# The last six token chunks of a sorted-attention and expert kernel, taken in pairs of 512 tokens

## The chip, the cores and the metric

The kernel runs on one core of a Trainium2 chip. Times are device microseconds of one execution. The profile is one further execution, recorded by the hardware profiler; its span runs from the first to the last instruction. In the texts PE is the matrix engine (TensorE), PEld its weight loads, DVE the vector engine, ACT the scalar engine, POOL GpSimd, and SP the engine whose queue issues most DMAs.

## The reference

Attention with sorted blocks comes first. Its result is the input of a layer of four experts, all of which see all tokens:

```python
# attention: q, k, v are (4, 8, 768, 64); P is an 8 x 8 Sinkhorn matrix per head
k_sorted = einsum('bhij,bhjcd->bhicd', P, k_blocks)      # v likewise
attn = softmax(scale * q_block @ k_sorted_block.T)       # within each block of 96
x = (attn @ v_sorted_block) as (3072 tokens, 512)

# experts: w1 is (4, 512, 1024), w2 is (4, 1024, 512)
p = domain_probs / (domain_probs.sum(-1, keepdims=True) + 1e-09)
for e in range(4):
    h = np.maximum(x @ w1[e], 0.0)
    out += p[:, e:e + 1] * (h @ w2[e])
```

## The kernel before

The 3072 tokens are taken in twelve chunks of 256, three for each of the four batches. A chunk goes through a first layer (x times w1, then Relu and the token's weight p, which gives the hidden values H in the buffer Hb) and a second layer (H times w2, summed over the four experts). The attention of batches 1 to 3 is woven into the chunks of the batch before. From chunk 6 on (G0 is 5, GN is 12) no attention is left, and all twelve matrices of input sums have been made, so TensorE has nothing but the two layers to do.

Both layers of these last chunks use Strassen's scheme in Winograd's form: a product of 2 x 2 blocks in seven block products in place of eight. In the second layer the two token blocks are the 128-token halves of a chunk, and the hidden values and the outputs are halved too. Sums of H blocks are made by the vector engine (h_sums, L747 to L753; into Sb, or in place over a block that is used up). In the first layer the blocks are two halves of 128 tokens, two halves of the 512 inputs and two halves of the 1024 hidden values. The sums on the weight side (s1, s3, n2, s4) were made earlier, in arena, in parts of Sb and over blocks of w1. Those on the token side (t1, n2, t3, t4) are four vector operations for each chunk, in token_sums (L1000), into the dead buffers kT and ET of the attention.

The function seven(g, e) returns the seven products of one expert as steps that are called by number. Each product has 4 blocks of 128 hidden values times 2 halves of the input, that is 8 matmuls of 128 columns, and fills one PSUM bank of 128 x 512 numbers. The product's line is L1047:

```python
dst[:, ds(f * P, P)], a[lhs][:, k, ds(f * P, P)], t[rhs][:, k, :],
```

Products are gathered in banks X, Z and Q. Product 1 goes to Z and is copied to X by ACT (L1067), since two sums start from it. Products 6 and 7 are added in X and copied out by ACT to u2 (L1074) and u3 (L1082). Product 2 completes Z and product 4 completes X, which the vector engine finishes with Relu and weight in one operation each (finish, L1053): these are the hidden values of the first token half. Product 3 and product 5 are in Q, to which the vector engine adds u3 (L1083) and u2 (L1091). ACT then takes the Relu (L1059) and GpSimd multiplies by the weight (finish2, L1060): these are the hidden values of the second token half.

The order on all engines is the order of the program (a manual schedule), written out in last_chunk (L1103 to L1217). An expert's step calls product 1 and 5 of its own, 2 and 6, with 7, 4 and 3 of the expert before among them. The second layer follows at L1161, and its products are the matmuls of L1150. The last steps of the first layer are called between its first products, and before its last product ends the next chunk has begun: token_sums(g + 1) at L1198 and last_begin(g + 1), with products 1 and 5 of the first expert, at L1203.

The weights p of a chunk are broadcast over the partitions by one DMA of 512 KB (load_p, L213) from SP's queue, issued at L1167, after the first product of the second layer. The tile pb has one buffer. Two output tiles, oa and ob, are taken for each chunk from a pool of two buffers (L1155). The first one to be written is oa, by the add at L1171. Stores are issued at L1206 (ob) and L1217 (oa), and for the last chunk also at L1173 and L1215.

last_tmp (L1015) lays the temporaries u2, u3, t22 and t12 into dead tiles: two buffers each for chunks 6 to 11. The transposed queries of the attention are in a pool tile qT with three buffers (L380).

Of the kernel before, what the change touches and what calls it, by code (L numbers as in the profile page):

```python
# [17 lines left out]
def kernel(  # L18
# [45 lines left out]

    state = {"n": 0}

# [181 lines left out]

    qTs = {}

    def warm(n):
# [127 lines left out]
    def st_q(b, pr):  # L379
        qT = att.tile([P, R, P], F16, name=f"qT_{b}_{pr}", tag="qT", bufs=3)  # L380
        nc.sync.dma_start_transpose(
            qT[:], natural[(b, "q")][:, pr].rearrange("p t h d -> p (t h d)")
        )
        qTs[(b, pr)] = qT.rearrange("p t x -> p (t x)").rearrange("p (i x) -> p i x", i=NB)
# [356 lines left out]

    def h_sums(e, which, own=False):
        blk = lambda kh, tok: Hb[:, homes.get(e, e), ds(kh * KH, KH), ds(tok * P, P)]
        sm = [Sb[:, n, e].rearrange("p (f x) -> p f x", f=KH) for n in range(4)]
        tt = nc.vector.tensor_tensor
        if which == 1:
            tt(sm[0], blk(0, 1), blk(1, 1), ALU.add)  # L747
        elif which == 2:
            tt(sm[1], sm[0], blk(0, 0), ALU.subtract)
        elif which == 3:  # L750
            tt(blk(0, 1) if own else sm[2], blk(0, 0), blk(0, 1), ALU.subtract)
        else:
            tt(blk(1, 0) if own else sm[3], blk(1, 0), sm[1], ALU.subtract)  # L753
# [231 lines left out]
    def token_sums(g, part=slice(0, 4)):  # L985
# [10 lines left out]
        for dst, x, y, op in (  # L996
# [3 lines left out]
            nc.vector.tensor_tensor(t[dst], t[x], t[y], op)  # L1000

    last = {}

    def last_banks(n):
# [10 lines left out]
    def last_tmp(g):  # L1015

        room = []
        if g > G0:
            t = moe.tile([P, NKC, NB, BLK], F16, name="tmp7", tag="xT").rearrange("p k i x -> p (k i x)").bitcast(F32)
            room += [t[:, ds(n * 512, 512)] for n in range(3)]  # L1020
        for m in range(2):
            t = att.tile([P, NB, 4, VW], F16, name=f"tmp7_{g}_{m}", tag="vs").rearrange("p i h w -> p (i h w)")
            t = t[:, 0:2048].bitcast(F32)
            room += [t[:, 0:512], t[:, 512:1024]]
        for m in range(1 if g > G0 else 2):
            t = att.tile([P, NB, 2, D], F16, name=f"tmp7x_{g}_{m}", tag="xsl").rearrange("p i h d -> p (i h d)")
            room.append(t.bitcast(F32))
        if g > G0:
            for n, nm in enumerate(("u2", "u3", "t22", "t12")):
                last[nm] = room[2 * n:2 * n + 2]  # L1030
        else:
            last["u2"] = last["t12"] = room[0::2]
            last["u3"] = last["t22"] = room[1::2]

    def seven(g, e):

        a, t, pb = As[e], Bs[g], pbs[divmod(g, R // 2)]
        n = e - (g == G0)
        X, Z = [last[nm][n % len(last[nm])][:] for nm in ("X", "Z")]
        u2, u3, t22, t12 = [last[nm][n % len(last[nm])] for nm in ("u2", "u3", "t22", "t12")]  # L1040
        Q = last["Q"][e if n == e else (0, 0, 1, 3)[e]][:]
        tt = nc.vector.tensor_tensor

        def product(dst, lhs, rhs, first=False):
            for f in range(KH):
                for k in range(2):
                    nc.tensor.matmul(  # L1047
                        dst[:, ds(f * P, P)], a[lhs][:, k, ds(f * P, P)], t[rhs][:, k, :],
                        start=(first and f == 0 and k == 0), stop=(f == KH - 1 and k == 1), skip_group_check=True,
                    )  # L1050

        def finish(i, j, src):
            nc.vector.scalar_tensor_tensor(  # L1053
                out=Hb[:, e, ds(i * KH, KH), ds(j * P, P)], in0=src.rearrange("p (f x) -> p f x", f=KH), scalar=0.0,
                op0=ALU.max, in1=pb[:, ds(e, 1), ds(j * P, P)].broadcast_to([P, KH, P]), op1=ALU.mult,
            )

        def finish2(i, j, src):
            nc.scalar.activation(src, src, AF.Relu, bias=0.0, scale=1.0)  # L1059
            nc.gpsimd.tensor_tensor(  # L1060
                Hb[:, e, ds(i * KH, KH), ds(j * P, P)], src.rearrange("p (f x) -> p f x", f=KH),
                pb[:, ds(e, 1), ds(j * P, P)].broadcast_to([P, KH, P]), ALU.mult,
            )
# [38 lines left out]

    def last_chunk(g, slot=None):  # L1103
        b, c = divmod(g, R // 2)
        final = g == GN - 1
        lead = int(g == G0)
# [13 lines left out]
        else:  # L1120
            last["e0"][2]()
            prs = {0: last["e0"]}
        for e in range(1 + lead, E):
            prs[e] = seven(g, e)
        for e in range(1 + lead, E):
            now, prev = prs[e], prs[e - 1]
# [11 lines left out]
        now[7]()  # L1138
        prev[12]()

        blk = lambda kh, tok: (lambda e, f: Hb[:, e, kh * KH + f, ds(tok * P, P)])
        sm = lambda n: (lambda e, f: Sb[:, n, e, ds(f * P, P)])
        bankB, bankA, bankC, bankQ = [last["Q"][n][:, 0:DH] for n in ((0, 2, 1, 3) if lead else range(4))]

        def product(ps, lhs, rhs, first=True, es=range(E), between=None, at=E - 1, part=ds(0, DH)):
            for e in es:
                if e == at and between:
                    between()
                for f in range(KH):
# [3 lines left out]
                    )  # L1153

        oa, ob = [moeo.tile([P, Dm], F32, name=f"{n}_{b}_{c}", tag="oacc") for n in ("oa", "ob")]  # L1155
        p1, p5, u2 = [moe.tile([P, DH], F32, name=f"{n}_{b}_{c}", tag=n, bufs=1) for n in ("p1", "p5", "u2")]
# [3 lines left out]

        product(bankA, blk(0, 0), "b11", between=now[4])  # L1161
        now[22]()
        nc.scalar.copy(p1[:], bankA)
        now[3]()
        now[12]()
        if not final:
            pbs[divmod(g + 1, R // 2)] = load_p(*divmod(g + 1, R // 2))  # L1167
        for e in range(E - 1):
            h_sums(e, 1)
        product(bankB, blk(1, 0), "b21")  # L1170
        tt(oa1, bankB, p1[:], ALU.add)  # L1171
        if final:
            nc.sync.dma_start(o[:, 2 * c, 0:DH], oa1)  # L1173
        h_sums(E - 1, 1)
        for e in range(E):
            h_sums(e, 2)
        product(bankC, blk(1, 1), "n4")
        nc.scalar.copy(ob1, bankC)
        for e in range(E):
            h_sums(e, 4, True)  # L1180
        if lead:
            for e in range(E):
                h_sums(e, 3, True)
            input_sums(0, 2, True)
# [6 lines left out]
        if not lead:  # L1191
            for e in range(E):
                h_sums(e, 3, True)
        early = 1 if final else 2
        for bank, part, _ in ends:
            product(bank[:, part], blk(1, 0), "b22", False, range(early), part=part)
        if not final:
            token_sums(g + 1)  # L1198
        product(bankA, blk(0, 1), "t3", False)
        if not final:  # L1200
            if lead:
# [7 lines left out]
        for bank, part, queue in ends:  # L1209
            product(  # L1210
                bank[:, part], blk(1, 0), "b22", False, range(early, E), None if final else last["e0"][6], 3, part
            )
# [127 lines left out]
    for g in range(G0 + 1):  # L1340
# [24 lines left out]
        else:  # L1365
            last_chunk(g, slot)
    for g in range(G0 + 1, GN):
        last_chunk(g)
# [28 lines left out]
```

## Time and profile before

| What | us |
|---|---|
| runs of the kernel | 363.46, 363.92, 370.13 (median 363.92) |
| the profiled execution | 362.61 |
| its span | 360.8 |
| PE busy | 353.0 |
| DVE busy | 277.3 |
| ACT busy | 173.6 |
| POOL busy | 133.9 |
| one chunk of the last six, in the trace | 24.70 |
| median time from issue to landing: weights p, stores of ob, stores of oa | 6.0, 2.0, 2.2 |

The page gives for every engine its busy time, and under it the share of each of 40 slices in tenths (9 is 90% or more); the PEclk row is TensorE's granted clock in tenths of full speed. The chain of work that ended last is followed back from the last instruction, at each step to what released it. A line of the timeline gives the start, the time until the last of the merged instructions ended, the engine, the line of the source, the operation, what it writes and reads, the count, and in brackets the idle time before and what ended it. Matmuls are pipelined, so their durations overlap, and the time of one is read from the distance of starts. A line of a stretch gives the stretch, its length, the busy time of PE, PEld, DVE, ACT and POOL with counts, the clock, the DMA share and the GB/s. Some matmul records can be missing from a trace.

### The profile page before, as it was taken

The numbers are of one execution on the slowest core, as the hardware profiler recorded it, in microseconds if no ns is written. First come the engines' busy times: TensorE is split into PE (matmuls) and PEld (weight loads), VectorE is DVE, ScalarE is ACT, GpSimd is POOL, SyncE is SP. The second block draws the span as 40 slices with busy tenths as digits, with TensorE's granted clock in tenths as the row PEclk, the third lists the DMA queues.
The fourth block names the chain that finished last, engine by engine and source line by source line (L and its number), as shares of the span: only waits on it lengthen the run. The fifth ranks groups of instructions, "written<-read, shape, count | busy, mean of one in ns | idle before, by whom it ended". The sixth has DMA issues, their size and how long they took to land.

```text
span 360.8 us, 10849 instructions
## 1 busy us (share of the span) xinstructions
PE 353.0 (98%) x4621; PEld 314.9 (87%) x4621; DVE 277.3 (77%) x561; ACT 173.6 (48%) x306; POOL 133.9 (37%) x148
## 2 busy tenths in 40 slices
PE   8799999999999999999999999999999999999996
PEld 8686857888888888988889899999999998999995
DVE  5653897779788777768878978869779679588695
ACT  2664430452324255368937257175283481571750
POOL 8872010466012330000626318147065082180470
PEclk9999999999999999999999999999999999999999
DMA  7999999999998999935995210210202203103101
GB/s 101 206 207 231 215 209 198 202 189 205 209 142 140 192 129 165 172 83 69 172 205 71 60 60 2 60 60 8 91 25 48 72 3 58 63 2 60 60 9 52
DMA packets 71964, 40.60 MB, mean 113 GB/s; under 512 B 40550, under 2 KB 66668, under 8 KB 71916
## 3 DMA queue, kind: packets, MB, share of 16 engines
q0 software_dynamic: 36560, 19.93, 41.0%
q1 hardware_dynamic: 35212, 19.92, 28.2%
q8 instruction: 36, 0.59, 0.7%
q14 instruction: 12, 0.10, 0.1%
q10 hardware_dynamic: 144, 0.07, 0.1%
HBM read 42.13 MB, written 6.34 MB: 134 GB/s over the span
## 4 chain that ended last, share of the span: by engine, by line
PE 91%; DVE 5%; ACT 1%; POOL 1%; issue 1%; DMA 0%; DVEq 0%; ACTq 0%; POOLq 0%
PE ps_Q L1150 24%; PE ps_h L777 18%; PE ps_X L1047 10%; PE ps_p L761 10%; PE ps_Z L1047 7%; PE ps_Q L1047 7%; PE ps_h L667 3%; PE ps_o L702 3%; PE ps_p L812 3%; PE ps_s L412 1%; PE ps_a L447 1%; PE ps_v L360 1%; PE ps_k L393 1%; PE ps_s L544 0%; DMA sn<-in_sort_net_dram 0%
## 5 line engine op out<-in xcount | busy, mean ns | idle before, releaser
L1060 POOL TENSOR_TENSOR Hb<-tmp,pb 128x512 f16<-128x512 f32 x40 | 50.7, 1275 | 84.7 <-ACT tmp L1059 83.3
L777 PE MATMUL ps_h<-xT,w 128*128 128x256 f16 x576 | 67.7, 273 | 0.0
L777 PEld LDWEIGHTS <-w 128*128 128x128 f16 x576 | 55.2, 98 | 7.3
L1150 PEld LDWEIGHTS <-Hb 128*128 128x128 f16 x576 | 53.8, 98 | 5.6
L783 DVE SCALAR_TENSOR_TENSOR Hb<-ps_h,pb 128x1024 f16<-128x1024 f32 x34 | 41.5, 1223 | 17.1 <-PE ps_h L777 16.8
L1047 PEld LDWEIGHTS <-w 128*128 128x128 f16 x864 | 52.4, 98 | 1.2 <-issue 0.3
L1150 PE MATMUL ps_Q<-w,Hb 128*128 128x256 f16 (+1 forms) x352 | 43.4, 268 | 0.0
L1047 PEld LDWEIGHTS <-arena 128*128 128x128 f16 x552 | 33.4, 98 | 0.1
L419 ACT ACTIVATE ET<-ps_s 96x768 f16<-96x768 f32 x24 | 18.0, 802 | 25.4 <-PE ps_s L412 25.1
L402 ACT CAST kT<-ps_k 64x384 f16<-64x384 f32 x48 | 22.7, 473 | 14.1 <-PE ps_k L393 13.1
L1047 PE MATMUL ps_X<-kT,arena 128*128 128x128 f16 x384 | 29.3, 219 | 0.0
L1067 ACT COPY ps_X<-ps_Z 128x512 f32<-128x512 f32 x27 | 15.4, 570 | 28.7 <-PE ps_Z L1047 28.3
L1083 DVE TENSOR_TENSOR tmp<-ps_Q,tmp 128x512 f32<-128x512 f32 x26 | 18.0, 691 | 14.2 <-ACT tmp L1082 10.0
L747 DVE TENSOR_TENSOR Sb<-Hb 128x512 f16<-128x512 f16 x45 | 27.7, 639 | 0.0
L1150 PE MATMUL ps_Q<-T,Hb 128*128 128x256 f16 x224 | 26.7, 273 | 0.0
L121 POOL DMA_DIRECT2D arena<-in_q_dram x24 | 19.9, 844 | 17.2 <-DMA qT<-arena 17.0
L1059 ACT ACTIVATE tmp<-tmp 128x512 f32<-128x512 f32 x40 | 25.4, 634 | 1.2 <-DVE tmp L1083 1.0
L761 PEld LDWEIGHTS <-Hb 128*128 128x128 f16 x232 | 21.9, 98 | 3.0
L1150 PEld LDWEIGHTS <-Sb 128*128 128x128 f16 x240 | 22.1, 98 | 2.4
L1074 ACT COPY tmp<-ps_X 128x512 f32<-128x512 f32 x26 | 15.2, 586 | 13.0 <-PE ps_X L1047 13.0
L1060 POOL TENSOR_TENSOR Hb<-tmp7x,pb 128x512 f16<-128x512 f32 x14 | 19.0, 1358 | 5.4 <-ACT tmp7x L1059 5.4
L1053 DVE SCALAR_TENSOR_TENSOR Hb<-ps_X,pb 128x512 f16<-128x512 f32 x27 | 18.4, 683 | 2.7 <-PE ps_X L1047 2.7
(206 smaller groups left out, 652.6 us busy)
## 6 DMA issues: line engine op xcount, KB each, us to landing
w<-in_moe_w_dram POOLq DMA_DIRECT2D x7, 1024.0 KB, 28.1
pb<-p_dram SPq DMA_DIRECT2D x12, 512.0 KB, 6.0
arena<-in_k_dram POOLq DMA_DIRECT2D x8, 384.0 KB, 9.4
arena<-in_v_dram POOLq DMA_DIRECT2D x8, 384.0 KB, 7.8
vs<-arena SPq DMA_DIRECT2D x36, 66.0 KB, 5.7
arena<-in_q_dram POOLq DMA_DIRECT2D x24, 96.0 KB, 8.4
out_dram<-ob SPq DMA_DIRECT2D x9, 256.0 KB, 2.0
out_dram<-oa SPq DMA_DIRECT2D x8, 256.0 KB, 2.2
```

Source lines behind the costliest of these rows:

```text
L121: nc.gpsimd.dma_start(t[:, h // 2, :, h % 2, :], q[b, h].rearrange("(t p) d -> p t d", p=P))
L402: nc.scalar.copy(kT[ds(D * hh, D), r], pk[ds(D * r, D), hh].rearrange("p a (i c) -> p a i c", c=CP),)
L419: nc.scalar.activation(ETs[2 * (pr % 2) + hh][:, 0:S].rearrange("c (a x) -> c a x", a=2), pss[hh][0:BLK, :, 0:HS], AF.Exp, bias=0.0, scale ...
L747: tt(sm[0], blk(0, 1), blk(1, 1), ALU.add)
L761: nc.tensor.matmul(ps, lhs(e, f), Ts[e][rhs][:, f, :], start=(first and e == es[0] and f == 0), stop=(done and e == es[-1] and f == KH - 1 ...
L777: nc.tensor.matmul(ps[:, f, :], w1sb[e][:, kc, ds((4 * g + f) * P, P)], xT[:, kc, ds(2 * c * P, 2 * P)], start=(kc == 0), stop=(kc == NKC ...
L783: nc.vector.scalar_tensor_tensor(out=Hb[:, homes.get(e, e), ds(4 * g, 4), :], in0=ps[:], scalar=0.0, op0=ALU.max, in1=weights(e).broadcast ...
L1047: nc.tensor.matmul(dst[:, ds(f * P, P)], a[lhs][:, k, ds(f * P, P)], t[rhs][:, k, :], start=(first and f == 0 and k == 0), stop=(f == KH - ...
L1053: nc.vector.scalar_tensor_tensor(out=Hb[:, e, ds(i * KH, KH), ds(j * P, P)], in0=src.rearrange("p (f x) -> p f x", f=KH), scalar=0.0, op0= ...
L1059: nc.scalar.activation(src, src, AF.Relu, bias=0.0, scale=1.0)
L1060: nc.gpsimd.tensor_tensor(Hb[:, e, ds(i * KH, KH), ds(j * P, P)], src.rearrange("p (f x) -> p f x", f=KH), pb[:, ds(e, 1), ds(j * P, P)].b ...
L1150: nc.tensor.matmul(ps, lhs(e, f), Ts[e][rhs][:, f, part], start=(first and e == 0 and f == 0), stop=(e == E - 1 and f == KH - 1), skip_gro ...
```

## The change

Chunks 6 to 11 are taken in pairs: (6, 7), (8, 9), (10, 11). In the first layer a pair is one block of 512 tokens, and its two token blocks are the two chunks. last_chunk is split into last_first (the first layer) and last_second (the second layer); a pair runs one last_first and then two last_seconds.

- seven(g, n) now stands for half an expert: expert n // 2 and two of the four blocks of hidden values. A product has 2 blocks times 2 input halves, 4 matmuls of 256 columns, and fills a bank of 512 as before. A pair has eight such steps. Chunk 5 (G0) keeps the 128-column form.
- The hidden values of the first chunk all come from the vector engine's finish and lie in Hb. Those of the second all come from ACT and GpSimd and lie in dead buffers: 2048 columns each of arena, of Sb's fourth part, of the query ring, and of an xT tile.
- pair_sums makes the four token sums once for each pair, with 512 elements in place of 256, at the place of token_sums in the second chunk's second layer.
- load_pair loads the weights of the first chunk with load_p and those of the second with two DMAs of 256 KB into xsl tiles. The extra DMAs are on SP's queue.
- last_tmp gives u2 with t12, and u3 with t22, three buffers each.
- The transposed queries go to a constant tile q_ring with three parts in place of the pool tile.
- The second last_second (upper) reads its blocks from the dead buffers, uses banks Z for two of its products, and has no steps of the first layer woven into its beginning.

The core of the diff:

```diff
 def st_q(b, pr):
-        qT = att.tile([P, R, P], F16, name=f"qT_{b}_{pr}", tag="qT", bufs=3)
+        qT = q_ring[:, state["q"] % 3]
+        state["q"] += 1
...
+    def pair_sums(g):
+        (x00, x10), (x01, x11) = halves(g)
+        own = lambda t: t[:, 0:4 * P].rearrange("p (k x) -> p k x", k=2)
+        t = Bs[g] = {
+            "b11": x00, "b12": x01, "b21": x10, "b22": x11,
+            "t1": own(kTs[0]), "n2": own(wide[0]), "t3": own(wide[2]), "t4": own(wide[3]),
+        }
...
+    def load_pair(g):
+        first, second = load_p(*divmod(g, R // 2)), []
+        b, c = divmod(g + 1, R // 2)
+        for n in range(2):
+            t = att.tile([P, NB, 2, D], F16, name=f"pb7_{g}_{n}", tag="xsl").rearrange("p i h d -> p (i h d)")
+            t = t.bitcast(F32).rearrange("p (e x) -> p e x", e=2)
+            nc.sync.dma_start(
+                t,
+                p_dram[ds(2 * n, 2), ds(b * S + 2 * c * P, 2 * P)].rearrange("(o e) x -> o e x", o=1).broadcast_to(
+                    [P, 2, 2 * P]
+                ),
+            )
+            second.append(t)
+        pbs[g] = lambda j, e: first[:, ds(e, 1), :] if j == 0 else second[e // 2][:, ds(e % 2, 1), :]
...
+            parts = (
+                arena[:, 4096:6144], Sflat[:, 6144:8192],
+                q_ring.rearrange("p n r x -> p (n r x)")[:, 0:2048], t[:, 0:2048],
+            )
+            last["H"] = [h.rearrange("p (f x) -> p f x", f=NFC) for h in parts]
...
+        last["u2"] = last["t12"] = room7[0::2]
+        last["u3"] = last["t22"] = room7[1::2]
...
+        else:
+            e, f0, cols = n // 2, n % 2 * 2, 2 * P
+            home = lambda i, j: (last["H"][e] if j else Hb[:, e])[:, ds(i * KH + f0, 2), :]
+            weight = lambda j: pbs[g](j, e)
+            Q = last["Q"][n % 4][:]
+        m = 512 // cols
...
-            for f in range(KH):
+            for f in range(m):
                 for k in range(2):
                     nc.tensor.matmul(
-                        dst[:, ds(f * P, P)], a[lhs][:, k, ds(f * P, P)], t[rhs][:, k, :],
+                        dst[:, ds(f * cols, cols)], a[lhs][:, k, ds((f0 + f) * P, P)], t[rhs][:, k, :],
...
+        N7 = E if lead else 2 * E
-        for e in range(1 + lead, E):
+        for e in range(1 + lead, N7):
             prs[e] = seven(g, e)
...
+    def last_second(g, now=None, upper=False):
+        closing = lead or upper
+        hb = (lambda e: last["H"][e]) if upper else (lambda e: Hb[:, e])
...
+        if upper:
+            bankA, bankB = last["Z"][1][:, 0:DH], last["Z"][0][:, 0:DH]
...
-        if not final:
-            token_sums(g + 1)
+        if closing and not final:
+            pair_sums(g + 1)
...
-    for g in range(G0 + 1, GN):
-        last_chunk(g)
+    for g in range(G0 + 1, GN, 2):
+        last_second(g, last_first(g))
+        last_second(g + 1, upper=True)
```

## The prediction

> **What bounds the kernel now.** I read the page first, for the engine that is never idle; then the chain that ended last; then busy times of the last chunks, for what one costs; then the timeline of one chunk, for the time per matmul and the slack of the engines behind TensorE.
>
> ```profile
> span 360.8 us, 10849 instructions
> PE 353.0 (98%) x4621; PEld 314.9 (87%) x4621; DVE 277.3 (77%) x561; ACT 173.6 (48%) x306; POOL 133.9 (37%) x148
> PE   8799999999999999999999999999999999999996
> PEclk9999999999999999999999999999999999999999
> PE 91%; DVE 5%; ACT 1%; POOL 1%; issue 1%; DMA 0%; DVEq 0%; ACTq 0%; POOLq 0%
> ```
>
> TensorE is busy from start to end at the full clock, and 91% of the chain is its matmuls. The stretches below are one chunk each (busy time by engine; x counts recorded instructions).
>
> ```profile
> 232.90:257.60 24.70, 24.70 (x338) 23.42 (x337) 19.43 (x40) 12.74 (x24) 10.32 (x8) 1.00 0.14 44
> 257.60:282.30 24.70, 24.70 (x338) 23.43 (x337) 19.43 (x40) 12.74 (x24) 10.32 (x8) 1.00 0.18 45
> ```
>
> TensorE has no gap in them. A change here gains only by fewer or cheaper matmuls, and loses what it makes TensorE wait. The time per matmul comes from TensorE's timeline, from starts far apart:
>
> ```profile
> 236.02 0.61 PE L1047 MATMUL ps_X<-kT,Sb 128*128 128x128 f16 x8
> ...
> 245.40 1.47 PE L1150 MATMUL ps_Q<-w,Hb 128*128 128x256 f16 x12
> ...
> 248.04 1.91 PE L1150 MATMUL ps_Q<-w,Hb 128*128 128x256 f16 x16
> ...
> 255.03 1.04 PE L1150 MATMUL ps_Q<-w,Hb 128*128 128x256 f16 x8
> ```
>
> From 236.02 to 245.40 lie 21 products of 8 first-layer matmuls: 9.38 / 168 = 55.8 ns each, 128 columns. From 248.04 to 255.03 lie 64 second-layer ones: 6.99 / 64 = 109.2 ns, 256 columns. So one of 256 is 2.4 ns cheaper than two of 128. The 219 and 273 ns of the groups are latencies of overlapped matmuls and are not used for the sum.
>
> One step of the first layer (about 3.13 us, one expert), all engines; the step begins at 238.70 with product 1 and the next at 241.83:
>
> ```profile
> 239.87 0.59 ACT L1082 COPY tmp<-ps_X 128x512 f32<-128x512 f32 x1
> 240.04 0.61 PE L1047 MATMUL ps_Z<-xT,w 128*128 128x128 f16 x8
> 240.50 0.69 DVE L1083 TENSOR_TENSOR tmp<-ps_Q,tmp 128x512 f32<-128x512 f32 x1 [0.69 <-ACT tmp L1082]
> 241.10 0.68 DVE L1053 SCALAR_TENSOR_TENSOR Hb<-ps_Z,pb 128x512 f16<-128x512 f32 x1
> 241.70 0.68 DVE L1053 SCALAR_TENSOR_TENSOR Hb<-ps_X,pb 128x512 f16<-128x512 f32 x1
> 241.83 0.61 PE L1047 MATMUL ps_Z<-xT,w 128*128 128x128 f16 x8
> 242.52 0.57 ACT L1067 COPY ps_X<-ps_Z 128x512 f32<-128x512 f32 x1 [0.21 <-PE ps_Z L1047]
> ```
>
> The copy at 242.52 overwrites the bank that the vector operation from 241.70 to 242.38 reads: it has 0.14 us of slack.
>
> **What the Trainium skill says.** "TensorE: Matmul & The Clock Gate", section "Wait — 56ns, not 53.3ns?": at the full clock a matmul takes N / 2.4 GHz plus a fixed 2.5 ns or so, whatever N. The trace agrees: 53.3 + 2.5 = 55.8 and 106.7 + 2.5 = 109.2. The same page, "Back-to-back issue gap", gives about 81 ns for N = 128 where each matmul has its own weight load; the trace doesn't agree (55.8 with a load each), and the measurement decides. "SBUF — State Buffer", section "SBUF: two separate sides": a vector operation with two SBUF inputs and a GpSimd operation lock each other out whole. The trace fits: three sums of L747 take 2.54 us (0.85 each) while GpSimd works, but 0.34 apart (1.42 for four of L749) when it doesn't.
>
> **The change, part by part.**
> *Matmuls.* Six chunks have 6 x 4 experts x 7 products x 8 = 1344 first-layer matmuls of 128 columns: 1344 x 55.8 = 75.06 us. The changed program has 672 of 256: 672 x 109.2 = 73.38. Gain 1.68 us, all on the path, as TensorE has no gap. Half the weight loads go as well; that they were hidden is shown by the pitch, so they add nothing. The second layer keeps its 816 matmuls.
> *Evacuations.* A product still fills one bank of 512 columns, so 8 steps of a pair stand for 2 x 4, each with the same two copies and one copy to X, two vector finishes (L1053), two vector adds and two Relu and GpSimd multiplies. Only operand shapes differ (2 x 256 for 4 x 128). Nearest row: 683 ns for L1053; the wide form of L783 with 256-column weight rows takes 1223 for 1024, so 540 for 512 more, no dearer per element. I take 683, with 640 to 750 for the range. GpSimd: 1275 ns taken, 1.2 to 1.45 us as bounds; two fit a step of 3.06 us at any of them.
> *The tighter step.* A step shrinks to 28 x 109.2 = 3.058 us. The loop that could bind it: copy to X, 0.48 to the next copy (243.00 after 242.52), 0.63 to the vector add (240.50 after 239.87), 0.60, 0.60, then 0.68 and some 0.05 of semaphore until the next copy to X: 3.04. It passes by about 0.02. Product 2 (240.04 after 238.70) waits for the same copy: 0.69 + 0.57 + 0.05 = 1.31 against 3 x 0.437 = 1.31. So the two are close enough that 0 to 0.05 us per step may be lost, 7 steps x 3 pairs: 0 to 1.0. I take 0.2. If the cover were gone (finishes at 750 ns) a step would be 3.18, a loss of 21 x 0.12 = 2.5 us. Below nothing is excluded, since matmul time is a floor.
> *Buffers u2, u3.* Three deep instead of two or so: the add at 243.69 waited for GpSimd (the operations ending 243.66), off TensorE's path. That wait goes; next is ACT's copy. Worth 0.
> *Token sums.* 4 operations of 512 elements once per pair, about 4 x 0.34 + 0.1 = 1.5 us, for 2 x 4 of 256 (1.0 us each, from 256.07 to 257.07). In the old place product 5 needs only the first, due 2.0 us after it starts: hidden. If not, 0.5 us x 3.
> *Weight loads.* Per pair 512 KB as before and two of 256 KB: the same bytes, 9 issues for 6 on SP's queue at 0.38 us. They are issued a second layer ahead (12 us; a 512 KB load lands in 6.0), ahead of output stores that come 7 us later on that queue. Taken as 10 us in all, they land before the first GpSimd multiply that needs them (12 + 3 us). Cost 0; if late, GpSimd alone falls behind, with 0.4 us per step to catch up.
> *q_ring and dead buffers.* No copies are added; the transposes into the ring keep their order and waits. Nothing is moved past POOL's queue. Cost 0.
> *Two second layers in a row.* The first now needs only VectorE's half of the hidden values, so its sums no longer wait for GpSimd. In the second, GpSimd is idle, so 16 sums take 16 x 0.34 = 5.4 us and the pair's sums 1.5, in 12.2 us of matmuls. The new wait: the second's first add (L1171) writes the oa buffer whose store was issued about 0.7 us after the first's last matmul (T); stores land 2.0 to 2.5 us later, T + 3.2. The add wants to start at T + 32 x 0.1092 + 0.27 = T + 3.77. Behind it on VectorE stands the fourth sum, then all others; TensorE needs that sum at T + 60 x 0.1092 = T + 6.55, 0.85 after the add starts. So the add may start as late as T + 5.7. Cost 0.
> *Sum:* -1.68 + 0.2 = about -1.5 us; the profiled execution goes from 362.61 (span 360.8 and 1.8 around it) to 361.1. The median shown, 363.92, stands 1.3 above that execution, 363.46 is the other near it, and 370.13 stands apart. Off the mean of the two near ones, 363.7, -1.5 gives 362.2; I say 362.1.
>
> **The rivals.**
> *The loop binds (the gain goes).* The step is held at about the old 3.13 us by the ACT and VectorE loop. For it: 0.02 us of computed slack. Against: every duration in it is of a busy step of before. Time: 363.7 - 1.68 + 21 x 0.07 = 363.5.
> *The store holds VectorE (slower).* In the second second layer the oa store is followed at once by 1 MB of weights; if it takes what the stores from room take in the busy part (6.7 us), it lands at T + 7.4, the add starts 1.7 us too late, and TensorE stands still at the fourth expert of product 5: 1.7 x 3 pairs = 5.1, so 362.1 + 5.1 = 367.2. It decides where landing passes 5 us from issue. Against: the stores of these chunks land in at most 2.5, DMA share is 0.14 to 0.18, and the last pair has no weights behind its store. It costs more than the gain from a delay of 0.56 per pair on.
> *The weight loads were the bound.* If the skill's 81 ns were true here the gain would be 1344 x 81 - 672 x 109 = 35.6 us, so 328. The measured 55.8 excludes it nearly. That the change doesn't do what it says is out: the built program has the 672 wide matmuls, and the 168 narrow ones of the chunk before.
>
> **How the numbers follow.** Forecast 0.76, loop 0.13, store or another new wait 0.10, weight loads 0.01. The forecast alone spans 360.6 (no loss, and the lower of the runs as base) to 363.6. Range: 360.6 to 365.6, which takes in the loop with its slow finishes (363.7 - 1.68 + 2.5 = 364.5) and a store that is a little late, and leaves out some 0.15. About 2% is what a measurement of this kernel can tell from no change: faster needs under 356.6 (0.01), slower over 371.2, a fifth of the store's case (0.02), within 0.97.
>
> **What would show it.** Right: first-layer matmuls at 109 ns, TensorE without gaps until the end, three pairs of about 48.9 us (24.46 + 24.46) for 49.4. Wrong in the loop: gaps ahead of product 2, or ACT's copy to X waiting for VectorE's finish instead of TensorE. Wrong in the store: L1171's successor waiting for a DMA, and gaps about 6 us into every second second layer. A slower GpSimd multiply, over 1.5 us, would make it wrong too.

## The result

| | before | after |
|---|---|---|
| median of 6 runs each, us | 363.86 | 363.74 |
| lowest and highest | 363.46, 370.13 | 363.48, 364.65 |
| the profiled execution | 362.61 | 363.48 |
| its span | 360.8 | 361.7 |

Executions of either kernel that took about 370 us had a lower granted clock (0.985 to 0.995), and the ratios below leave them out. The ratio of the times is 1.0001, with an interval of 0.9985 to 1.0016: the change does nothing that can be measured. A forecast gain of 1.5 us (0.4%) would show in an interval of this width, and it isn't there. With 22 runs of the changed kernel against 59 of before on one chip (the first experiment) the ratio was 1.0019, with an interval of 1.0003 to 1.0035, so if anything it loses some 0.7 us. Below, such an interval stands in brackets behind its ratio.

The page of the changed kernel, with the lines that answer to those of before:

```profile
span 361.7 us, 9496 instructions
PE 352.7 (98%) x3949; PEld 305.5 (84%) x3949; DVE 271.8 (75%) x549; ACT 172.6 (48%) x306; POOL 133.6 (37%) x148
PE   8799999999999999999999999999999999999995
PEclk9999999999999999999999999999999999999999
```

TensorE has 672 matmuls fewer, is as busy by this count as before, and the clock is full. Neither the busy share nor the slices show where a gain of 1.7 us went: matmuls overlap, and a short gap between their starts is no idle time in them. The stretches of the three pairs, each in two parts, cut 0.4 us before the first matmul of the second layers:

```profile
208.44:232.94 24.50, 24.50 (x223) 21.50 (x221) 19.03 (x34) 19.19 (x36) 14.76 (x12) 1.00 0.06 23
232.94:257.82 24.88, 24.88 (x230) 22.31 (x228) 18.92 (x47) 5.94 (x13) 5.82 (x5) 1.00 0.21 65
257.82:282.32 24.50, 24.50 (x223) 21.49 (x221) 18.00 (x31) 19.20 (x36) 14.69 (x12) 1.00 0.06 22
282.32:307.20 24.88, 24.88 (x230) 22.30 (x228) 19.30 (x47) 5.93 (x13) 5.80 (x5) 1.00 0.26 65
307.20:331.64 24.44, 24.44 (x222) 21.49 (x220) 17.94 (x30) 19.13 (x36) 14.64 (x12) 1.00 0.06 23
331.64:357.93 26.29, 26.22 (x270) 23.56 (x268) 18.58 (x46) 6.16 (x15) 5.94 (x5) 1.00 0.07 26
```

Each of the first two pairs takes 24.50 + 24.88 = 49.38 us, where two chunks took 49.40 before. At 109.2 ns its 448 matmuls would take 48.92. So 0.46 us are lost in each pair, and one step of the first layer shows where. In this timeline of the changed kernel L1104 is the product, L1124 the copy to X, L1139 the copy to u3, L1140 the add of u3, and L1110 finish; lines of other operations in between are left out.

```profile
224.19 0.57 ACT L1124 COPY ps_X<-ps_Z 128x512 f32<-128x512 f32 x1 [0.29 <-DVE Hb L1110]
224.25 0.60 PE L1104 MATMUL ps_Q<-kT,arena 128*128 128x256 f16 x4
224.67 0.59 ACT L1139 COPY tmp<-ps_X 128x512 f32<-128x512 f32 x1
224.81 0.60 PE L1104 MATMUL ps_Z<-xT,w 128*128 128x256 f16 x4
225.24 0.60 PE L1104 MATMUL ps_X<-ET,arena 128*128 128x256 f16 x4
225.36 0.69 DVE L1140 TENSOR_TENSOR tmp<-ps_Q,tmp 128x512 f32<-128x512 f32 x1 [0.69 <-ACT tmp L1139]
225.68 0.60 PE L1104 MATMUL ps_X<-ET,w 128*128 128x256 f16 x4
225.97 0.68 DVE L1110 SCALAR_TENSOR_TENSOR Hb<-ps_Z,pb 128x512 f16<-128x512 f32 x1
226.11 0.60 PE L1104 MATMUL ps_Q<-xT,w 128*128 128x256 f16 x4
226.55 0.60 PE L1104 MATMUL ps_Z<-xT,w 128*128 128x256 f16 x4
226.57 0.68 DVE L1110 SCALAR_TENSOR_TENSOR Hb<-ps_X,pb 128x512 f16<-128x512 f32 x1
226.99 0.60 PE L1104 MATMUL ps_X<-ET,arena 128*128 128x256 f16 x4
227.36 0.57 ACT L1124 COPY ps_X<-ps_Z 128x512 f32<-128x512 f32 x1 [0.29 <-DVE Hb L1110]
227.42 0.60 PE L1104 MATMUL ps_Q<-kT,arena 128*128 128x256 f16 x4
227.98 0.49 PE L1104 MATMUL ps_Z<-xT,w 128*128 128x256 f16 x3
```

From 224.81 to 226.99 are five products of four matmuls: 2.18 / 20 = 109 ns each, as forecast. But product 2 starts 0.56 us after product 5 (224.81 after 224.25, 227.98 after 227.42), where a product takes 0.437. The step is 3.17 us from product 2 to product 2. The copy to X, on which product 2 depends, is released by VectorE, not by TensorE: that is the loop of the prediction (copy to X, copy to u3, add, two finishes, next copy to X), and its length has become the step's. The first three steps of a pair are shorter, 3.06 to 3.10. In the list of waits of the whole program the same edge is, before and then after:

```profile
ACT ps_X L1067 <- PE ps_Z L1047: 28.3, 26, 4.7
```

```profile
ACT ps_X L1124 <- PE ps_Z L1104: 15.6, 11, 4.7
ACT ps_X L1124 <- DVE Hb L1110: 4.3, 16, 0.3
```

Before, the copy waited 26 times for TensorE; now 16 of its waits end with VectorE.

The layers are 149.49 us from the first pair's first product (208.44) to the last matmul (357.93), 149.69 before (208.18 to 357.87), so 0.20 us remain of the gain. The span is 0.87 longer all the same, so 1.07 us are lost outside them. The first product of the pairs starts 0.26 later than that of chunk 6 before. From the last matmul to the end of the span it is 3.77 us, and 2.96 before: 0.81 us that the prediction has no term for.

### The profile page after: what moved, and what is told of

Its sections match the earlier page's. It is cut to its first block, busy times and chain, and to the rows that moved or that the text cites. A ratio compares the mean times of both kernels' runs of the same rounds, so it can differ in the third digit from the quotient of the medians.

```text
span 361.7 us, 9496 instructions
## 1 busy us (share of the span) xinstructions
PE 352.7 (98%) x3949; PEld 305.5 (84%) x3949; DVE 271.8 (75%) x549; ACT 172.6 (48%) x306; POOL 133.6 (37%) x148
## 4 chain that ended last, share of the span: by engine, by line
PE 87%; DMA 6%; DVE 3%; POOL 1%; SPq 1%; ACT 1%; issue 1%; ACTq 0%; DVEq 0%; POOLq 0%
PE ps_Q L1217 17%; PE ps_h L780 16%; PE ps_X L1104 10%; PE ps_p L764 8%; PE ps_Z L1104 7%; PE ps_Q L1104 7%; PE ps_Z L1217 6%; DMA w<-in_moe_w_dram 4%; PE ps_h L669 3%; PE ps_o L704 3%; PE ps_p L815 3%; DMA vs<-arena 2%; PE ps_a L449 1%; PE ps_s L414 1%; PE ps_v L361 1%; SPq L375 1%
## 5 line engine op out<-in xcount | busy, mean ns | idle before, releaser
L780 PEld LDWEIGHTS <-w 128*128 128x128 f16 x576 | 55.2, 98 | 7.3
L1104 PEld LDWEIGHTS <-w 128*128 128x128 f16 x480 | 43.5, 98 | 6.4 <-issue 0.3
L1117 POOL TENSOR_TENSOR arena<-tmp,pb 128x512 f16<-128x512 f32 x12 | 15.3, 1276 | 65.8 <-PE ps_Z L1104 49.9
L1217 PEld LDWEIGHTS <-Hb 128*128 128x128 f16 x320 | 31.2, 98 | 3.6
L1217 PEld LDWEIGHTS <-Sb 128*128 128x128 f16 x304 | 28.2, 98 | 3.0
L1104 PEld LDWEIGHTS <-arena 128*128 128x128 f16 x312 | 27.7, 98 | 2.9
L1104 PE MATMUL ps_X<-ET,arena 128*128 128x256 f16 x168 | 25.2, 272 | 0.0
L1124 ACT COPY ps_X<-ps_Z 128x512 f32<-128x512 f32 x27 | 15.4, 570 | 19.9 <-PE ps_Z L1104 15.6
L764 PEld LDWEIGHTS <-Hb 128*128 128x128 f16 x232 | 21.9, 98 | 3.0
L1217 PE MATMUL ps_Q<-w,Hb 128*128 128x256 f16 x192 | 24.4, 273 | 0.0
L1104 PE MATMUL ps_Z<-xT,w 128*128 128x256 f16 (+1 forms) x176 | 22.5, 258 | 0.2 <-ACT ps_X L1124 0.2
L1140 DVE TENSOR_TENSOR tmp<-ps_Q,tmp 128x512 f32<-128x512 f32 x20 | 13.8, 692 | 11.3 <-ACT tmp L1139 7.6
L1110 DVE SCALAR_TENSOR_TENSOR Hb<-ps_X,pb 128x512 f16<-128x512 f32 x27 | 18.4, 682 | 1.6 <-PE ps_X L1104 1.6
L750 DVE TENSOR_TENSOR Sb<-Hb 128x512 f16<-128x512 f16 x33 | 19.5, 609 | 0.0
L1110 DVE SCALAR_TENSOR_TENSOR Hb<-ps_Z,pb 128x512 f16<-128x512 f32 x27 | 18.4, 682 | 1.3 <-PE ps_Z L1104 1.3
```

The lines of the kernel that those rows point to most:

```text
L764: nc.tensor.matmul(ps, lhs(e, f), Ts[e][rhs][:, f, :], start=(first and e == es[0] and f == 0), stop=(done and e == es[-1] and f == KH - 1 ...
L780: nc.tensor.matmul(ps[:, f, :], w1sb[e][:, kc, ds((4 * g + f) * P, P)], xT[:, kc, ds(2 * c * P, 2 * P)], start=(kc == 0), stop=(kc == NKC ...
L1104: nc.tensor.matmul(dst[:, ds(f * cols, cols)], a[lhs][:, k, ds((f0 + f) * P, P)], t[rhs][:, k, :], start=(first and f == 0 and k == 0), st ...
L1110: nc.vector.scalar_tensor_tensor(out=home(i, j), in0=src.rearrange("p (f x) -> p f x", f=m), scalar=0.0, op0=ALU.max, in1=weight(j).broadc ...
L1124: nc.scalar.copy(X, Z)
L1217: nc.tensor.matmul(ps, lhs(e, f), Ts[e][rhs][:, f, part], start=(first and e == 0 and f == 0), stop=(e == E - 1 and f == KH - 1), skip_gro ...
```

## The experiments

The theories, as the expectations name them. A: the loop of ACT and VectorE sets the step. B: GpSimd, which frees the buffers of u2 and u3, sets it. C: the loss is in the second layers. D: the constant query ring moves the attention's tiles and slows its transfers. E: the wait in the attention varies by itself. F, G and H are about the end of the program: F, the order in which it waits for DMAs when it closes; H, a fetch of instructions; G, something else.

**The changed kernel again.** No edit; the control for what follows, on its chip.

> The changed kernel again, as the base for the three that follow. Both theories: 363.7 us, the same as the kernel before; a pair's first layer has steps that grow from 3.06 to 3.17 us, and TensorE loses about 0.5 us per pair ahead of product 2.

Measured: 364.15 us against 363.17 for before, ratio 1.0019 [1.0003, 1.0035]; the first pair is 49.39 us, as in the profile above.

**The two finishes in the other order.** VectorE completes X first, so the copy to X of the next step finds its bank free one operation (0.60 us) earlier. Nothing is added or left out.

```diff
-        def p2():
+        def p2(done=True):
             product(Z, "a12", "b21")
-            finish(0, 0, Z)
+            if done:
+                finish(0, 0, Z)
...
-            22: lambda: finish2(1, 1, t22), 12: lambda: finish2(0, 1, t12),
+            20: lambda: finish(0, 0, Z), 22: lambda: finish2(1, 1, t22), 12: lambda: finish2(0, 1, t12),
...
-            now[2]()
+            now[2](bool(lead))
             now[6]()
             prev[22]()
             prev[4]()
+            if not lead:
+                now[20]()
             prev[3]()
```

Step 4 is product 4 with the finish of X; the finish of Z, which stood ahead of it with product 2, now follows it.

> The changed kernel with the two finishes of a step in the other order on VectorE: product 4's of the half-expert before ahead of product 2's. Theory A (the loop copy to X, copy to u3, add of u3, two finishes, next copy to X is longer than TensorE's step): the loop is cut, since the next copy to X waits for a finish that no longer stands behind the other; steps of 3.06 us, no gaps ahead of product 2, 1.4 us less: 362.3. Rival B (GpSimd is late with the buffers of the add of u3): the add stays as late as it was, but nothing waits for it, so 362.3 to 363.7. Rival C (the time is lost outside the first layer, in the two second layers in a row or the stores): no change, 363.7.

Measured: the step is 3.06 us, and the first pair 48.95 (from 208.96 to 257.91). Product 2 of two steps in a row, and the waits of the copy to X:

```profile
225.12 0.60 PE L1104 MATMUL ps_Z<-xT,w 128*128 128x256 f16 x4
...
228.18 0.60 PE L1104 MATMUL ps_Z<-xT,w 128*128 128x256 f16 x4
```

```profile
ACT ps_X L1124 <- PE ps_Z L1104: 18.0, 26, 4.7
```

26 are on TensorE again, as before, which is Theory A's mark. The layers take 148.23 us (208.96 to 357.19), 1.5 less than before and 1.3 less than in the changed kernel. The time was 363.26 us, ratio to before 1.001 [0.999, 1.003]: less than the unedited kernel on the same chip (364.15, ratio 1.0019), but no gain on before. The gaps are settled; something else of about the same size stands in the way.

**A fourth buffer for u3.** This takes away only the wait of the add for GpSimd. The engines wait for each other by semaphores, counters that an operation raises when it ends; an add that needs ACT and GpSimd waits for two of them.

```diff
-        last["u3"] = last["t22"] = room7[1::2]
+        last["u3"] = last["t22"] = room7[1::2] + ([Sflat[:, ds(2048, 1024)].bitcast(F32)] if g > G0 else [])
```

> The changed kernel with four buffers for u3 and t22 in place of three, the fourth in Sb's second part, which is idle in the first layer. The adds of u3 then wait for ACT alone instead of ACT and GpSimd. Theory A with a second wait that costs 0.07 us as such: steps of 3.10 us instead of 3.17 in the later part of a pair, so about 0.25 us per pair and 0.7 in all less: 363.0. Rival B (GpSimd's work is late): with a buffer more the whole loss goes, steps of 3.06, 362.3. Rival C: 363.7.

Measured: the pair is 49.18 us (209.17 to 258.35), the steps are 3.10 to 3.11 after a first of 3.06, and the time 363.45, ratio 1.0002 [0.9979, 1.0026]. One step of it, without TensorE and GpSimd:

```profile
224.85 0.57 ACT L1124 COPY ps_X<-ps_Z 128x512 f32<-128x512 f32 x1 [0.22 <-DVE Hb L1110]
225.33 0.59 ACT L1139 COPY tmp<-ps_X 128x512 f32<-128x512 f32 x1
225.95 0.69 DVE L1140 TENSOR_TENSOR tmp<-ps_Q,tmp 128x512 f32<-128x512 f32 x1 [0.62 <-ACT tmp L1139]
226.56 0.68 DVE L1110 SCALAR_TENSOR_TENSOR Hb<-ps_Z,pb 128x512 f16<-128x512 f32 x1
227.16 0.68 DVE L1110 SCALAR_TENSOR_TENSOR Hb<-ps_X,pb 128x512 f16<-128x512 f32 x1
227.95 0.57 ACT L1124 COPY ps_X<-ps_Z 128x512 f32<-128x512 f32 x1 [0.22 <-DVE Hb L1110]
```

The add starts 0.03 us after the copy that releases it (225.92 to 225.95). In the changed kernel it starts 0.10 after (225.26 to 225.36), although it waits for GpSimd's operation of three steps before. So GpSimd isn't late (B falls): it is the second wait as such that costs. The trace of the changed kernel has a semaphore instruction of 21 ns on VectorE's queue just there (225.30), ahead of the add. It is absent in the first three steps of each pair, and there the add starts 0.03 after the copy. Where it is present, in the last six chunks of this trace and of that of before, the add starts 0.10 after, whether the last operation of GpSimd ended 0.04 us earlier or 1.3. Two adds of before, with the copy and the GpSimd operations ahead of each:

```profile
241.07 2.59 POOL L1060 TENSOR_TENSOR Hb<-tmp,pb 128x512 f16<-128x512 f32 x2 [0.55 <-ACT tmp L1059]
243.00 0.59 ACT L1082 COPY tmp<-ps_X 128x512 f32<-128x512 f32 x1
243.69 0.69 DVE L1083 TENSOR_TENSOR tmp<-ps_Q,tmp 128x512 f32<-128x512 f32 x1 [0.71 <-POOL Hb L1060]
244.20 1.28 POOL L1060 TENSOR_TENSOR Hb<-tmp7x,pb 128x512 f16<-128x512 f32 x1 [0.54 <-ACT tmp7x L1059]
245.60 0.58 ACT L1082 COPY tmp<-ps_X 128x512 f32<-128x512 f32 x1 [0.17 <-PE ps_X L1047]
246.29 0.69 DVE L1083 TENSOR_TENSOR tmp<-ps_Q,tmp 128x512 f32<-128x512 f32 x1
```

The Trainium skill knows the instruction: "Perfetto Trace Analysis", section "Identifying Dependency Chains", has it that an instruction waiting for several engines may get semaphore instructions ahead of it. What one costs in the loop is shown here: 3.17 - 3.10 = 0.07 us per step. The rest of A stands, as the copy to X still waits for VectorE.

**Both edits.**

> The changed kernel with the finishes in the other order and the fourth buffer. Theory A: as with the order alone, steps of 3.06 us and 362.3, since TensorE's own pace is then the limit and the second wait is hidden. Rival B: 362.3. Rival C: 363.7.

Measured: steps of 3.06, a pair of 48.94, 363.31 us, ratio 0.9993 [0.9973, 1.0013]. With the finishes swapped the buffer shortens neither the step nor the pair.

**Before, once more, and with single parts of the change.** The first run is the kernel before on its new chip; then the ring alone; then the swap alone.

```diff
+    q_ring = const.tile([P, 3, R, P], F16, name="q_ring")
...
-        qT = att.tile([P, R, P], F16, name=f"qT_{b}_{pr}", tag="qT", bufs=3)
+        qT = q_ring[:, state["q"] % 3]
+        state["q"] += 1
```

> The kernel before once more, for a second profile of it. If the longer way to the first pair (TensorE waits 1.2 to 1.4 us for a store of v into vs in the attention, 0.5 in the first profile of before) and the longer end (3.8 us from the last matmul to the end of the span, 2.9 in the first profile of before) come from the day and not from the change, this profile shows a wait of about 1.2 us and an end of about 3.8. If they come from the change, it shows 0.5 and 2.9 again.

> The kernel before with only the query ring as a constant tile, in place of the pool tile; the last six chunks are as before. Theory D (the ring moves the other tiles to other addresses and makes the attention's DMAs slower): 0.7 to 1 us slower than before, with the wait for vs at 1.2 us or more. Theory E (the wait for vs varies by itself): the same as before.

> The kernel before with the two finishes of a step in the other order. Theory A (the loop of ACT and VectorE binds at 3.10 to 3.17 us a step): nothing, since four steps of 3.13 us with 128 columns have no gap before product 2 in the trace. Same as before, no change in the steps. If the order of the finishes were a gain of another kind, it would be 0.5 us or more faster here too.

Measured: 362.78 for the first, in one execution; with the ring 363.77, ratio 1.0003 [0.9989, 1.0017]; with the swap 364.11, ratio 1.0011 [0.9995, 1.0028]. With the swap the steps are 3.13 us as they were: the copy to X waited for TensorE there, so the swap has nothing to shorten. The ring costs nothing that can be measured. From the last matmul to the end of the span the three profiles have 2.94, 2.96 and 2.92 us, so the longer end comes from the change and not from the day.

**The swap, with the ring in the attention's pool.** It is one tile of the pool in place of a constant one, meant to leave the other tiles of the attention at their addresses of before. The finishes are swapped as above.

```diff
-        qT = q_ring[:, state["q"] % 3]
+        if state["q"] == 0:
+            state["ring"] = att.tile([P, 3, R, P], F16, name="q_ring", tag="qT", bufs=1)
+        qT = state["ring"][:, state["q"] % 3]
...
```

> The changed kernel with the finishes in the other order, and with the query ring as one tile of the attention pool in the place of the old tiles, so that the other tiles stand where they stood before. Theory D: the gain of the last six chunks comes through, 1.4 us less than before. Theory E: like the kernel with the finishes in the other order alone, within 0.5 us of before.

Measured: 363.12 us, ratio 0.9984 [0.997, 0.9998]: 0.6 us less than before, where D expected 1.4 and E at most 0.5. The wait in the attention is the one at this line, where TensorE stands still for the sorted values (here in the second profile of the changed kernel):

```profile
124.53 0.64 PE L449 MATMUL ps_a<-vs,ET 96*128 96x65 f16 x16 [1.44 <-DMA vs<-arena]
```

It is 1.38 in this kernel, without the constant ring, and absent in before with it: D falls. Over all profiles it is 0, 0, 0.3 and 0.5 in the four that have before's last chunks, and 0, 0.4, 0.6, 0.65, 1.2 and 1.4 (four times) in the nine that have the pairs. Only the ring differs in the program ahead of it. The changed kernel itself has 0.4 in one profile and 1.4 in the other, so it does vary by itself, as E has it. Whether the change makes the long wait more frequent is open: at a granted clock of 0.998 or more, the first product of the pairs starts at 207.9 to 209.7 us in eight profiles, that of chunk 6 at 208.2 to 208.4 in three.

**The end of the program.** After the last matmul there is one more add, its store, the store's landing, and the close, in which SP waits for the semaphores of the DMAs one after the other. The DMA view of the last microseconds gives the queue, its kind, packets, MB and share of the 16 DMA engines' time, and then the store with its size and the us from issue to landing. Before:

```profile
q1 hardware_dynamic: 288, 0.33, 20.5%
q10 hardware_dynamic: 144, 0.07, 4.7%
out_dram<-oa SPq DMA_DIRECT2D x1, 64.0 KB, 1.7
```

and after:

```profile
q1 hardware_dynamic: 288, 0.33, 20.7%
q10 hardware_dynamic: 144, 0.07, 5.0%
q14 instruction: 1, 0.01, 0.5%
out_dram<-oa SPq DMA_DIRECT2D x1, 64.0 KB, 2.2
```

A block of 8 KB of instructions is fetched by DMA 1.04 us after the last store's issue, while it is under way, and that store lands 0.5 us later than before. Before, the last fetch on this queue came at 344.34, 14 us ahead of the store. The trace has 461 entries for ACT before and 451 after, and at its last fetch ACT stands at its 444th before and its 448th after: it fits a block of ACT's that is now reached only at the end. Theory H is that this fetch delays the landing, and twelve tiny copies on ACT, in second layers where it is idle, test it:

```diff
         nc.scalar.copy(p1[:], bankA)
+        for _ in range(6 if upper and not final else 0):
+            nc.scalar.copy(p1[:, 0:1], p1[:, 0:1])
```

The other part: the DMAs of SP and the one of ACT take eight semaphores in turn, and the close waits for the semaphores in order. The trace of before has 104 of these DMAs, 13 rounds of eight, and the last store has the last semaphore. The change makes 107, so the last store has the third, and the waits for five others follow after it, 0.06 us apart though all five had been raised before. Theory F is that these five lengthen the close, and five DMAs more, 112 or 14 rounds, put the last store back on the last semaphore. (The expectation counts one more each time, 105, 108 and 113; the steps between them are the same.)

```diff
-            nc.sync.dma_start(
-                t,
-                p_dram[ds(2 * n, 2), ds(b * S + 2 * c * P, 2 * P)].rearrange("(o e) x -> o e x", o=1).broadcast_to(
-                    [P, 2, 2 * P]
-                ),
-            )
+            w = 2 if n and g == G0 + 1 else 1
+            for i in range(0, 2, w):
+                nc.sync.dma_start(
+                    t[:, ds(i, w), :],
+                    p_dram[ds(2 * n + i, w), ds(b * S + 2 * c * P, 2 * P)].rearrange("(o e) x -> o e x", o=1)
+                    .broadcast_to([P, w, 2 * P]),
+                )
```

> The changed kernel with five more DMAs on SP's queue: the loads of the second chunk's weights are split by expert, so that 113 DMAs stand for 108 and the last store falls on the last of the eight semaphores of SP's DMAs again, as it did with the 105 of before. Theory F (part of the end's loss is the order in which SP waits for those semaphores when the program closes): from the landing of the last store to the end of the span 0.9 us, as before, where the changed kernel has 1.2; the landing itself stays at 2.2 us after its issue; last matmul to end 3.5 in place of 3.8. Rival G (the close takes longer for another reason, such as a later end of another engine): 1.2 and 3.8 as they are. The first layer isn't touched: pairs of 49.4 us.

> The changed kernel with twelve copies of one column more on ACT, in the second layers of chunks 7 and 9, where ACT has nothing to do. Theory H (the last store lands 0.5 us later because ACT's next block of instructions is fetched by DMA just then, and the change, with ten fewer instructions on ACT, moved that fetch there from 14 us before): the fetch on the instruction queue goes to an earlier place, the last store lands 1.7 us after its issue as before, and last matmul to end is 3.3 in place of 3.8. Rival G (the fetch has nothing to do with the landing, or isn't ACT's): landing at 2.2 and end at 3.8. The first layer isn't touched: pairs of 49.4 us.

> The changed kernel with the order of the two finishes swapped on VectorE, the five DMAs and the twelve copies, all three at once. Theories A, F and H together: pairs of 48.95 us, last matmul to end 2.95; 1.3 us of matmul time and 0.85 of the end won against the changed kernel, so about 361.6 to 362.2 in time, 0.995 to 0.998 of before; the wait for the sorted values in the attention (0.4 to 1.4 us) stays in it, as nothing here touches it. Rival G: pairs of 48.95, end 3.8, time as with the swap alone, 1.000 of before.

Measured, in us of the profiled executions:

| | last store, issue to landing | landing to end of span | last matmul to end |
|---|---|---|---|
| before | 1.68 | 0.93 | 2.96 |
| after | 2.19 | 1.23 | 3.77 |
| five DMAs more | 2.22 | 0.92 | 3.50 |
| twelve copies more | 1.70 | 1.23 | 3.29 |
| both, and the swap | 1.72 | 0.92 | 3.00 |

Each edit moves its own column to the value of before and leaves the other alone, so F and H hold and G falls. The columns hardly vary otherwise: over all four profiles with before's chunks the last matmul to the end is 2.92 to 2.96, over the six with pairs and neither edit of the end 3.76 to 3.88. With the five DMAs, which add nothing on ACT, the fetch stays 1.08 us behind the store's issue. With the copies it is at 349.6 and gone from the end:

```profile
q1 hardware_dynamic: 288, 0.33, 20.4%
q10 hardware_dynamic: 144, 0.07, 4.7%
out_dram<-oa SPq DMA_DIRECT2D x1, 64.0 KB, 1.7
```

One execution of each took 362.71 us (DMAs) and 363.21 (copies); single times are too rough for 0.3 us. The kernel with all three edits gave 362.13 us against 363.38 for before, with a ratio of 0.9964 [0.9947, 0.9981]. Its pairs:

```profile
209.41:258.35 48.94, 48.94 (x451) 43.82 (x448) 38.88 (x79) 26.38 (x54) 20.40 (x16) 1.00 0.17 44
258.35:307.30 48.95, 48.95 (x451) 43.84 (x449) 37.91 (x76) 26.37 (x54) 20.38 (x16) 1.00 0.17 44
307.30:357.58 50.28, 50.21 (x490) 45.07 (x487) 37.45 (x75) 25.38 (x49) 20.37 (x16) 1.00 0.07 25
```

The layers take 148.17 us, 1.52 less than before: the gain of the wide matmuls, now kept. This version is 1.3 us (0.4%) faster than before; the changed kernel wasn't run beside it, but was no faster than before in either of its two measurements.

## Why the prediction was wrong

The range held the time (363.74 in 360.6 to 365.6), the forecast gain didn't come. The loop of ACT and VectorE took back 1.32 us where 0.2 were allowed, and the end of the program, which has no term in the sum, grew by 0.81. By the prediction's steps:

- *Matmuls.* Right, with a sum that is a little large. 109 ns was measured, and 1.52 us were there once nothing stood in the way. 1344 x 55.8 is 75.00 and not 75.06, so the gain by the prediction's own figures is 1.62 and not 1.68; and two chunks of before measured 49.40 where these figures give 49.46.
- *Evacuations.* Right in the durations: finish 0.68, copy 0.57 and 0.59, add 0.69, GpSimd 1.28 us. It spoke of the operations and not of ACT's count of instructions, ten fewer in the trace, with which the fetch came to the end: 0.5 us.
- *The tighter step.* **This step failed.** The loop was taken at 3.04 us, 0.02 under the step of 3.058, with 0.2 us of loss. It measured 0.48 + 0.69 + 0.61 + 0.60 + 0.79 = 3.17. Two terms were mis-sized. The hand-over, from the end of the finish on VectorE to the start of ACT's copy that waits for it, was taken as 0.05 and is 0.11 (227.25 to 227.36). From ACT's copy to the add was taken as 0.63 from a step of before, and is 0.69 from the fourth step of a pair on, where the add waits for two engines. That start was in the trace of before (243.69 after 243.00), but was read as GpSimd's being late. With only the first in force the loop is 3.10, as the fourth buffer shows. The loss in the three pairs is (49.38 + 49.38 + 50.73) - (48.94 + 48.95 + 50.28) = 1.32 us, against a bound of 1.0 that the prediction gave for it. Before hid the first: there the copy waited for TensorE, so the 0.14 us from the finish to the copy (242.38 to 242.52) was taken for slack, with the hand-over inside it: the slack was 0.03.
- *Buffers u2, u3.* Wrong in its reading. GpSimd's end at 243.66 was a coincidence: the next add of before (246.29, shown above) starts as long after its copy, and GpSimd had then been done for 0.81 us. Three buffers leave the second wait in place, and its 0.07 us are on the path as soon as the loop binds.
- *Token sums*, *q_ring and dead buffers*, *Two second layers in a row.* Right, at nothing that can be measured. A pair from its second layer on has no gap, and no store holds VectorE. C falls with that: the swap alone brought the pair to 48.95.
- *Weight loads.* Right in the stretch they were argued for, but three more DMAs cost 0.3 us at the close, by the order of its waits. "Cost 0" looked only at the place where they are issued.
- The rivals: "the loop binds" came true, at 363.5 for 363.74, with 0.13 of the chance. It should have had more: the margin was 0.02 us, and no row of before showed the hand-over from VectorE to ACT while it was the limit. That its figure is so near is in part luck: it holds every step at 3.13, where the later ones became 3.17 and the earlier ones 3.06 to 3.10, and it has nothing for the 0.81 us of the end.

The balance of the profiled executions: start of the pairs +0.26, layers -0.20, end +0.81, sum +0.87 us, which is 363.48 - 362.61. The layers are -1.52 of wide matmuls and +1.32 of gaps. Of the 0.26, the wait in the attention explains nothing (0.4 after, 0.5 before). TensorE also waits 0.74 us for a load of w at 19.16 in the profile after and not in that of before; but such waits for DMAs in the first 60 us come and go, from 0 to 2.0 us in all, in profiles of either kind.

This is the balance of two executions, and that of before lies 1.25 us under its median of 363.86. What repeats from profile to profile is the layers and the end, -0.2 + 0.8 = +0.6 us; the two measurements gave 0.0 (from -0.5 to +0.6) and +0.7 (from +0.1 to +1.3). For the swap the same sum gives -1.5 + 0.8 = -0.7 us against before, and the ratios gave +0.4 (from -0.4 to +1.1) for the swap alone, -0.3 (from -1.0 to +0.5) with the fourth buffer and -0.6 (from -1.1 to -0.1) with the ring in the pool. The first of them leaves 1.1 us unexplained; the wait in the attention, 1.2 in its profile, may be a part, which isn't shown.

## What to carry to other kernels

When a step gets shorter, sum the loop of the other engines with its hand-overs, each measured where the waiting engine had nothing else to wait for, and take a margin of hundredths of a microsecond for none. Here the cure was the order of two operations on the engine behind: the reader whose buffer is needed first goes first. A gain of under one per cent has to be followed to the end of the program too: here three more DMAs and ten fewer instructions on one engine put 0.81 us between the last matmul and the end.

## What the runs showed of the hardware

- A second wait on an operation of VectorE cost 0.07 us even where GpSimd had been done for 1.3 us: the add starts 0.10 us after its releaser in place of 0.03.
- The hand-over from VectorE's finish to ACT's copy took 0.11 us (227.25 to 227.36), from ACT's copy to VectorE's add, with one wait, 0.03 (225.92 to 225.95).
- With a fetch of 8 KB of instructions during the last store, the store landed 2.2 us after its issue in place of 1.7; twelve copies more on ACT, earlier, moved the fetch away, and the store landed after 1.7 us again.
- The close of the program waits for its eight DMA semaphores in order: with the last store on the third of them in place of the eighth, five waits of 0.06 us follow its landing, and from the landing to the end of the span it took 1.23 us in place of 0.93.
